# Moving the second look at two groups' decays, with its loads, to the last two groups with attention

## The chip, the cores and the metric

The kernel runs on one core of a Trainium2 chip. Its time is in device microseconds (us) and is the median of three runs of the same program. One more execution was recorded by the profiler; all rows below come from that one.

A core has five engines, each of which takes its instructions in the order in which they were written for it: TensorE (PE; PEld is its loading of weights), VectorE (DVE), ScalarE (ACT), GpSimd (POOL) and SyncE (SP). Here SP does nothing but issue DMA transfers. An instruction that waits for a semaphore holds up everything behind it on its own engine.

## The reference, cut to what matters

```python
def _attn_ref(q, k, v, alpha):            # 4 batches, 8 heads, 768 steps, 48 channels
    for t in range(S):
        state = alpha[:, :, t, :, None] * state + np.einsum('bhd,bhe->bhde', k[:, :, t], v[:, :, t])
        y[:, :, t] = np.einsum('bhd,bhde->bhe', q[:, :, t], state)

def _moe_ref(x, w_a, w_b, w_out):         # 3072 tokens, 384 -> 1536 -> 384
    return (x @ w_a) * (x @ w_b) @ w_out

def _moe2_ref(x, modality_id, w_gate, modality_bias, w1, w2):   # 8 experts, one per token
    e_idx = np.argmax(x @ w_gate + modality_bias[modality_id], axis=1)
    for e in range(E):
        h = np.maximum(x[e_idx == e] @ w1[e], 0.0)
        out[e_idx == e] = gate_w * (h @ w2[e])

def reference(...):
    y = _attn_ref(q, k, v, alpha)         # a linear attention whose state decays by alpha
    return _moe2_ref(_moe_ref(y, ...), ...)
```

## The kernel before, in words

The 3072 tokens are cut into eight groups of 384 (`NW` = 8, `WIN` = 384), and a group into three chunks of 128 (`CPW` = 3). For a group `w` the class `Attention` computes the decayed attention: a chunk's rows of alpha, k and q are loaded into tiles `raw_a`, `raw_k`, `raw_q` (eight buffers, tag "raw"), turned on DVE into `at`, `kt`, `qt`, scanned along time, and multiplied on PE: `s` are the scores, `y` the result, `u` what goes into `state`. `moe(w)` then computes the gated product of the group in twelve blocks: eighteen matmuls give `ab` (nine for each of the two factors), DVE multiplies the two factors into `g` (L632), ACT and DVE split `g` into `gh` and `gl`, and nine matmuls add to `px`. The bank of the second factor has one buffer, so the nine matmuls of the next block's second factor can't begin before DVE has read the present one into `g`.

While `moe(w)` runs, the main loop also steps through `Attention(w + 1)` and `route(w - 1)`, which picks each token's expert. From group 1 on a scheduler orders the instructions of each engine, and so it also starts a group's first chunks ahead of time: `at6_1` (group 6, chunk 1) stands beside `moe(4)`. After the eight groups the experts run, each with weights that are loaded once the routes are known.

The scans are exact only while each decay lies within 1.0 - 0.375 and 1.0 + 0.375. So every decay is also compared with these limits: `guard` (L268 and L269) takes the least and the greatest of a tile into the columns of `amin` and `amax`, and `spans()` later makes a flag of them, on which a general path hangs. For the groups 2 to 7 this is done on `at`. For the groups 0 and 1 (`LATE` = 2) it is done later: `late_guard` loads their alpha a second time in four tiles of two heads each (128 partitions of 288 numbers, 144 KB) and reduces each twice. Before, this stands at the end of the last chunk of the groups 2 and 3, beside `moe(1)` and `moe(2)`. Its tiles have the tag "sm", three buffers that the masked scores (`sm`) and the turned keys (`ktok`) use as well.

Of the kernel before, what the change touches and what calls it, by code (L numbers as in the profile page):

```python
# [10 lines left out]
F32 = mybir.dt.float32  # L11
# [4 lines left out]
ALU = mybir.AluOpType  # L16
AX = mybir.AxisListType
# [3 lines left out]
P = 128  # L21
WIN = 384
CPW = WIN // P
# [4 lines left out]
LATE = 2  # L28
# [16 lines left out]
def gla_moe_kernel(ctx, tc, q, k, v, alpha, w_a, w_b, w_out, modality_id, w_gate, modality_bias, w1, w2, out):  # L45
    nc = tc.nc
    B, H, S, D = q.shape
# [7 lines left out]
    NW = N // WIN  # L55
    WPB = S // WIN
    NPAIR = H // 2
# [66 lines left out]
    amin = const.tile([P, NW * NPAIR], F32, name="amin")  # L124
    nc.gpsimd.memset(amin, 1.0)
    amax = const.tile([P, NW * NPAIR], F32, name="amax")
# [21 lines left out]
    ap = m2 = fold = None  # L148
# [89 lines left out]
    def after_first(steps):  # L238

        gl, w = newest["gl"].ins, newest["w"].ins  # L240
        while True:
            with tc.issue_after(gl), tc.issue_after(w):
                try:
                    next(steps)
                except StopIteration:
                    return
            yield

    def behind(steps):

        while True:
            with tc.issue_after(newest["mm"].ins):
                try:
                    next(steps)
                except StopIteration:
                    return
            yield
# [8 lines left out]
    def guard(i, a):  # L266
        axis = AX.X if len(a.shape) == 2 else AX.XY
        nc.vector.tensor_reduce(amin[:, i : i + 1], a, axis=axis, op=ALU.min)  # L268
        nc.vector.tensor_reduce(amax[:, i : i + 1], a, axis=axis, op=ALU.max)  # L269

    def late_guard(w):

        b, t0 = w // WPB, (w % WPB) * WIN
        for i in range(NPAIR):
            r = ap.tile([P, 4 * P], F32, tag="sm", bufs=3, name=f"late{w}_{i}")[:, : 2 * CPW * D]
            nc.sync.dma_start(
                out=r.rearrange("p (h f) -> p h f", h=2),
                in_=alpha[b, 2 * i : 2 * i + 2, t0 : t0 + WIN, :].rearrange("h (p j) d -> p h (j d)", j=CPW),
            )
            guard(w * NPAIR + i, r)  # L280

    class Attention:

# [229 lines left out]
        def steps(self):  # L513
            w = self.w
            if w != 1:
                self.load(0)
            self.load(1)
            yield
            yield from self.prepare(0)
            for c in range(CPW):  # L520
                self.scores(c)
                yield
                ahead = self.prepare(c + 1) if c + 1 < CPW else iter(())
                yield from islice(ahead, 1)
                self.mask(c)
                yield
                yield from ahead
                self.pads(c)
                self.decay(c)
                self.values(c)  # L530
                self.halves(c)
                yield
                if self.gc(c) < S // P - 1:
                    self.keys(c)
                    self.carry(c)
                    self.add(c)
                if c == CPW - 1 and LATE <= w < 2 * LATE:
                    late_guard(w - LATE)
                yield

        def first(self, beside, second):
# [869 lines left out]
```

## Time and profile before

| | |
|---|---|
| median of three runs | 882.64 us (879.58 to 885.08) |
| the profiled execution, its own time | 880.6 us |
| its span, first to last instruction | 878.6 us |
| mean granted clock of TensorE | 0.987 of full speed |
| PE busy | 837.5 us (95%) |
| DVE busy | 633.7 us (72%) |
| ACT, POOL busy | 291.4 us (33%), 201.2 us (23%) |
| HBM read and written | 100.10 MB, 9.82 MB |

A share of busy time is a mean over stages with different limits. The groups take the span up to about 640 us, the experts the rest.

### The profile page before, as it was taken

Reading aid. Unit: us, or ns where it says so; the run is one execution under the profiler, and the core shown is the slowest. Engines: PE = TensorE matmul, PEld = TensorE weight load, DVE = VectorE, ACT = ScalarE, POOL = GpSimd, SP = SyncE. Lnnn points to the kernel's source line nnn. Section 1 sums busy time; section 2 is a strip of 40 time slices with the busy share of each in tenths; the row PEclk is TensorE's granted clock in tenths of the full one; section 3 lists DMA queues with packets and bytes.
Section 4 is the critical chain, followed back from the end, with each engine's and each line's share of the span. In section 5 each row is a group of like instructions: output and inputs, shape, how many; then the busy total and the mean of one; then the engine's idle time right before and its main releaser. Section 6 shows DMA issues by size and latency. Waiting matters only on the chain.

```text
span 878.6 us, 16754 instructions
## 1 busy us (share of the span) xinstructions
PE 837.5 (95%) x6220; PEld 782.4 (89%) x6220; DVE 633.7 (72%) x1457; ACT 291.4 (33%) x681; POOL 201.2 (23%) x273
## 2 busy tenths in 40 slices
PE   7879889989999999999999999999999999999995
PEld 6767789989998999989899998999999998998994
DVE  7799889974686888499698666356568965775651
ACT  2323332212221222222122122122465565555541
POOL 5011101120020102011100201011416554455431
PEclk9989999999999999999999999999999999999998
DMA  9989757332233313024120000100772988695810
GB/s 174 201 194 198 167 150 215 86 84 58 64 81 74 89 49 81 28 64 108 45 65 10 1 28 1 72 28 1 263 251 84 354 284 308 195 358 169 289 56 23
DMA packets 124928, 110.98 MB, mean 126 GB/s; under 512 B 55759, under 2 KB 104051, under 8 KB 124836
## 3 DMA queue, kind: packets, MB, share of 16 engines
q1 hardware_dynamic: 114548, 99.00, 40.6%
q0 software_dynamic: 4032, 9.62, 3.1%
q10 hardware_dynamic: 6256, 1.19, 1.1%
q8 instruction: 51, 0.84, 0.4%
q14 instruction: 41, 0.34, 0.1%
HBM read 100.10 MB, written 9.82 MB: 125 GB/s over the span
## 4 chain that ended last, share of the span: by engine, by line
PE 70%; DVE 13%; DMA 7%; issue 4%; POOL 2%; ACT 2%; SPq 2%; POOLq 0%; DVEq 0%; ACTq 0%
PE ab L625 26%; PE px L616 12%; PE hl L1055 8%; PE pol L1003 8%; PE s L404 3%; PE he L1055 2%; PE poe L1003 2%; DMA wa<-in_moe_w_a 2%; PE u L493 2%; DVE g L632 1%; DMA tab_d<-fill 1%; DVE at L390 1%; DVE R L379 1%; PE k L485 1%; PE y L452 1%
## 5 line engine op out<-in xcount | busy, mean ns | idle before, releaser
L625 PE MATMUL ab<-xh,pb 128*128 128x384 f32 x576 | 167.9, 345 | 10.1 <-DVE g L632 10.0
L625 PE MATMUL ab<-xh,pa 128*128 128x384 f32 x576 | 166.3, 342 | 3.4 <-DVE pa L196 2.4
L616 PE MATMUL px<-po,gh 128*128 128x384 f32 x576 | 139.6, 342 | 3.4 <-ACT gh L634 3.1
L634 ACT ACTIVATE gh<-g 128x384 fp32r<-128x384 f32 x96 | 50.3, 524 | 232.4 <-DVE g L632 223.6
L625 PEld LDWEIGHTS ab<-xh,pb 128*128 128x128 f32 x576 | 106.5, 189 | 15.5 <-DVE g L632 12.0
L625 PEld LDWEIGHTS ab<-xh,pa 128*128 128x128 f32 x576 | 105.5, 188 | 7.7 <-DVE pa L196 3.3
L632 DVE TENSOR_TENSOR g<-ab,asb 128x384 f32<-128x384 f32 x96 | 53.1, 553 | 79.2 <-PE ab L625 73.2
L616 PEld LDWEIGHTS px<-po,gh 128*128 128x128 f32 x576 | 104.3, 191 | 5.6 <-ACT gh L634 4.1
L625 PE MATMUL ab<-xl,pb 128*128 128x384 f32 x288 | 97.4, 338 | 0.0
L625 PE MATMUL ab<-xl,pa 128*128 128x384 f32 x288 | 97.1, 337 | 0.0
L630 ACT ACTIVATE asb<-ab 128x384 f32<-128x384 f32 x96 | 46.9, 489 | 146.8 <-PE ab L625 146.8
L616 PE MATMUL px<-po,gl 128*128 128x384 f32 x288 | 86.8, 340 | 0.0
L392 POOL TENSOR_TENSOR qt<-qt,at 128x512 f32<-128x512 f32 x18 | 22.2, 1235 | 254.0 <-DVE qt L358 201.5
L638 DVE TENSOR_TENSOR gl<-g,gh 128x384 fp32r<-128x384 f32 x96 | 56.2, 585 | 21.5 <-ACT gh L634 21.3
L1060 DVE SCALAR_TENSOR_TENSOR hll<-hl,hhl 128x256 fp32r<-128x256 f32 x72 | 30.3, 421 | 56.8 <-ACT hhl L1058 51.9
L671 DVE SCALAR_TENSOR_TENSOR junk<-xr,gate 128x384 bf16<-128x384 f32 x96 | 54.1, 564 | 4.8 <-ACT xr L648 3.2
L625 PEld LDWEIGHTS ab<-xl,pb 128*128 128x128 f32 x288 | 54.6, 190 | 0.1
L625 PEld LDWEIGHTS ab<-xl,pa 128*128 128x128 f32 x288 | 54.3, 188 | 0.3 <-DVE xl L479 0.2
L616 PEld LDWEIGHTS px<-po,gl 128*128 128x128 f32 x288 | 52.6, 188 | 1.0 <-issue 0.6
L437 POOL TENSOR_TENSOR state<-state,R 128x384 f32<-128x384 f32 x18 | 17.5, 970 | 135.6 <-DVE state L509 67.4
L1058 ACT ACTIVATE hhl<-hl 128x256 fp32r<-128x256 f32 x72 | 27.7, 384 | 62.1 <-PE hl L1055 53.0
L404 PE MATMUL s<-qt,kt 64*128 64x128 f32 x384 | 41.6, 298 | 4.7 <-DVE qt L392 3.9
(332 smaller groups left out, 1840.5 us busy)
## 6 DMA issues: line engine op xcount, KB each, us to landing
w1rl<-in_moe_w SPq DMA_DIRECT2D x18, 768.0 KB
w2rl<-in_moe_w SPq DMA_DIRECT2D x18, 768.0 KB
raw_a<-in_alpha SPq DMA_DIRECT2D x72, 96.0 KB
raw_k<-in_k SPq DMA_DIRECT2D x72, 96.0 KB
raw_q<-in_q SPq DMA_DIRECT2D x72, 96.0 KB
wo<-in_moe_w_out SPq DMA_DIRECT2D x6, 768.0 KB
x_d<-xr SPq DMA_DIRECT2D x24, 192.0 KB
w1re<-in_moe_w SPq DMA_DIRECT2D x6, 768.0 KB
```

The costliest lines, as they stand in the source:

```text
L404: nc.tensor.matmul(pts[g][:, i * P : (i + 1) * P], kt[o : o + 64, i, :], qt[o : o + 64, i, :], start=True, stop=True)
L616: newest["mm"] = nc.tensor.matmul(px[t][:, :DM], a_, b_, start=(f == 0 and i == 0), stop=(f == NF - 1 and i == 2))
L625: nc.tensor.matmul(pt[:, :WIN], a_, b_, start=(n == 0), stop=(n == 3 * KD - 1))
L630: nc.scalar.activation(asb, pt[:, :WIN], AF.Copy)
L632: nc.vector.tensor_tensor(g, pab[1][:, :WIN], asb, op=ALU.mult)
L634: newest["act"] = nc.scalar.activation(gh, g, AF.Copy)
L638: newest["gl"] = nc.vector.tensor_tensor(gl, g, gh, op=ALU.subtract)
L671: nc.vector.scalar_tensor_tensor(junk, xr[w][t], 1.0, gate[e], op0=ALU.mult, op1=ALU.mult, accum_out=L[:, t, e : e + 1])
L1003: newest["mm"] = nc.tensor.matmul(self.po[t][:, :DM], a_, b_, start=(f == 0 and i == 0), stop=(f == NF2 - 1 and i == 2))
L1055: nc.tensor.matmul(pt[:, :n], a_, b_, start=(i == 0), stop=(i == 3 * KD - 1))
L1058: nc.scalar.activation(gh[:, :n], pt[:, :n], AF.Relu)
L1060: nc.vector.scalar_tensor_tensor(gl[:, :n], pt[:, :n], 0.0, gh[:, :n], op0=ALU.max, op1=ALU.subtract)
```

## The change

The function `late_guard` is parted. `late_load` now loads two tiles of four heads each (128 partitions of 2 times 288 numbers, 288 KB) into buffers of the rows (tag "raw", eight of them, which don't grow), and `late_guard` reduces each tile twice, into two columns at once. The loads stand at the end of chunk 1, the reductions at the end of chunk 2, and both stand in the groups 6 and 7 in place of 2 and 3. Eight loads become four and sixteen reductions eight; the bytes stay the same.

```diff
--- before.py
+++ after.py
@@ -268,16 +268,25 @@
         nc.vector.tensor_reduce(amin[:, i : i + 1], a, axis=axis, op=ALU.min)
         nc.vector.tensor_reduce(amax[:, i : i + 1], a, axis=axis, op=ALU.max)
 
-    def late_guard(w):
+    def late_load(w):
 
         b, t0 = w // WPB, (w % WPB) * WIN
-        for i in range(NPAIR):
-            r = ap.tile([P, 4 * P], F32, tag="sm", bufs=3, name=f"late{w}_{i}")[:, : 2 * CPW * D]
+        ts = []
+        for i in range(NPAIR // 2):
+            r = ap.tile([P, 2, 2 * CPW * D], F32, tag="raw", bufs=8, name=f"late{w}_{i}")
             nc.sync.dma_start(
-                out=r.rearrange("p (h f) -> p h f", h=2),
-                in_=alpha[b, 2 * i : 2 * i + 2, t0 : t0 + WIN, :].rearrange("h (p j) d -> p h (j d)", j=CPW),
+                out=r.rearrange("p a (h f) -> p (a h) f", h=2),
+                in_=alpha[b, 4 * i : 4 * i + 4, t0 : t0 + WIN, :].rearrange("h (p j) d -> p h (j d)", j=CPW),
             )
-            guard(w * NPAIR + i, r)
+            ts.append(r)
+        return ts
+
+    def late_guard(w, ts):
+
+        for i, r in enumerate(ts):
+            cols = slice(w * NPAIR + 2 * i, w * NPAIR + 2 * i + 2)
+            nc.vector.tensor_reduce(amin[:, cols], r, axis=AX.X, op=ALU.min)
+            nc.vector.tensor_reduce(amax[:, cols], r, axis=AX.X, op=ALU.max)
 
     class Attention:
 
@@ -534,8 +543,11 @@
                     self.keys(c)
                     self.carry(c)
                     self.add(c)
-                if c == CPW - 1 and LATE <= w < 2 * LATE:
-                    late_guard(w - LATE)
+                if w >= NW - LATE:
+                    if c == CPW - 2:
+                        late = late_load(w - NW + LATE)
+                    elif c == CPW - 1:
+                        late_guard(w - NW + LATE, late)
                 yield
 
         def first(self, beside, second):
```

What the scheduler makes of it, at three places. The names carry the group first: `late0_1` is the second tile for group 0, `at3_2` the decays of group 3, chunk 2, `g1_9` the product of block 9 of `moe(1)`.

DVE beside `moe(1)`, before the change: the last rows up to the product `g1_9` (the least of `late0_0` and the turning of `at3_2` stand just ahead of them).

```order
L269 TENSOR_REDUCE amax_122<-late0_0_2090 128x1
L268 TENSOR_REDUCE amin_120<-at3_2_2646 128x1
L268 TENSOR_REDUCE amin_120<-late0_1_2094 128x1
L269 TENSOR_REDUCE amax_122<-late0_1_2094 128x1
L269 TENSOR_REDUCE amax_122<-at3_2_2646 128x1
L509 TENSOR_TENSOR state_133<-u2_2_2081,state_133 64x4x32
L509 TENSOR_TENSOR state_133<-u2_2_2081,state_133 64x4x16
L509 TENSOR_TENSOR state_133<-u2_2_2081,state_133 64x4x32
L509 TENSOR_TENSOR state_133<-u2_2_2081,state_133 64x4x16
L268 TENSOR_REDUCE amin_120<-late0_2_2098 128x1
L269 TENSOR_REDUCE amax_122<-late0_2_2098 128x1
L632 TENSOR_TENSOR g1_9_2202<-ab1_9_1_2192,asb1_9_2190 128x384
```

DVE at the same place now:

```order
L367 STREAM_TRANSPOSE at3_2_2630<-raw_a3_2_2386 128x4x4x32
L268 TENSOR_REDUCE amin_120<-at3_2_2630 128x1
L269 TENSOR_REDUCE amax_122<-at3_2_2630 128x1
L379 TENSOR_SCALAR at3_2_2630<-at3_2_2630 128x4x128
L518 TENSOR_TENSOR state_133<-u2_2_2081,state_133 64x4x32
L518 TENSOR_TENSOR state_133<-u2_2_2081,state_133 64x4x16
L518 TENSOR_TENSOR state_133<-u2_2_2081,state_133 64x4x32
L518 TENSOR_TENSOR state_133<-u2_2_2081,state_133 64x4x16
L644 TENSOR_TENSOR g1_9_2186<-ab1_9_1_2176,asb1_9_2174 128x384
```

The reductions on late tiles are gone from here (six of the eight stood ahead of `g1_9`, two a little behind it); beside `moe(2)` eight more go in the same way.

DVE beside `moe(4)`, before the change: from the turning of `qt6_0` to the product of block 6.

```order
L358 STREAM_TRANSPOSE qt6_0_4815<-raw_q6_0_4741 128x4x4x32
L358 STREAM_TRANSPOSE kt6_0_4777<-raw_k6_0_4736 128x4x4x32
L479 TENSOR_TENSOR xl5_3934<-y5_1_4310,xh5_3933 128x3x128
L358 STREAM_TRANSPOSE at6_1_4845<-raw_a6_1_4748 128x4x4x32
L388 TENSOR_TENSOR kt6_0_4777<-kt6_0_4777,R6_0_4771 128x512
L268 TENSOR_REDUCE amin_120<-at6_1_4845 128x1
L269 TENSOR_REDUCE amax_122<-at6_1_4845 128x1
L376 MEMSET R6_1_4851 128x2
L632 TENSOR_TENSOR g4_6_4458<-ab4_6_1_4448,asb4_6_4446 128x384
```

DVE at the same place now, from the turning of `kt6_0` (which stands right behind `qt6_0`):

```order
L367 STREAM_TRANSPOSE kt6_0_4745<-raw_k6_0_4704 128x4x4x32
L488 TENSOR_TENSOR xl5_3902<-y5_1_4278,xh5_3901 128x3x128
L367 STREAM_TRANSPOSE at6_1_4813<-raw_a6_1_4716 128x4x4x32
L397 TENSOR_TENSOR kt6_0_4745<-kt6_0_4745,R6_0_4739 128x512
L288 TENSOR_REDUCE amin_120<-late0_0_5108 128x2
L289 TENSOR_REDUCE amax_122<-late0_0_5108 128x2
L268 TENSOR_REDUCE amin_120<-at6_1_4813 128x1
L269 TENSOR_REDUCE amax_122<-at6_1_4813 128x1
L385 MEMSET R6_1_4819 128x2
L288 TENSOR_REDUCE amin_120<-late0_1_5110 128x2
L289 TENSOR_REDUCE amax_122<-late0_1_5110 128x2
L644 TENSOR_TENSOR g4_6_4426<-ab4_6_1_4416,asb4_6_4414 128x384
```

Four reductions on `late0` now stand ahead of `g4_6`. Beside `moe(5)` the four on `late1` stand in the same way ahead of `g5_6`, behind the turning of `at7_1`.

SP at that place, before the change:

```order
L333 DMA raw_q6_2_4828<-in_q 32x4x192 x4
L318 DMA v6_1_4763<-in_v 128x8x48
L333 DMA raw_a7_0_5534<-in_alpha 32x4x192 x4
L333 DMA raw_k7_0_5539<-in_k 32x4x192 x4
L333 DMA raw_q7_0_5544<-in_q 32x4x192 x4
L318 DMA v6_2_4833<-in_v 128x8x48
L333 DMA raw_a7_1_5551<-in_alpha 32x4x192 x4
```

SP at that place now:

```order
L342 DMA raw_q6_2_4796<-in_q 32x4x192 x4
L327 DMA v6_1_4731<-in_v 128x8x48
L277 DMA late0_0_5108<-in_alpha 128x4x144
L277 DMA late0_1_5110<-in_alpha 128x4x144
L342 DMA raw_a7_0_5510<-in_alpha 32x4x192 x4
L342 DMA raw_k7_0_5515<-in_k 32x4x192 x2
L327 DMA v6_2_4801<-in_v 128x8x48
L342 DMA raw_k7_0_5515<-in_k 32x4x192 x2
L342 DMA raw_q7_0_5520<-in_q 32x4x192 x4
```

The two loads of `late0` stand ahead of the rows of group 7. In the built program `late0_0` waits for the turning of `qt6_0` and `late0_1` for that of `kt6_0`, which free the buffers that they get; `raw_a7_0`, which got the first of these before, now waits for the turning of `at6_1`. The loads of `late1` wait in the same way for `qt7_0` and `kt7_0`.

## Rows read from the trace of the kernel before

**Rows 1.** The page, part 1 (busy time, share, instructions) and part 4 (the chain)

```profile
PE 837.5 (95%) x6220; PEld 782.4 (89%) x6220; DVE 633.7 (72%) x1457; ACT 291.4 (33%) x681; POOL 201.2 (23%) x273
...
PE 70%; DVE 13%; DMA 7%; issue 4%; POOL 2%; ACT 2%; SPq 2%; POOLq 0%; DVEq 0%; ACTq 0%
```

**Rows 2.** Idle of TensorE on the product, whole span, then 180 to 300 us

```profile
PE ab L625 <- DVE g L632: 10.0, 7, 3.4
...
PE ab L625 <- DVE g L632: 5.5, 2, 3.4
```

**Rows 3.** Timeline of PE at its two restarts: start, length, engine, line

```profile
198.87 0.44 PE L625 MATMUL ab<-xh,pb 128*128 128x384 f32 x1 [3.42 <-DVE g L632]
...
271.94 0.69 PE L625 MATMUL ab<-xh,pb 128*128 128x384 f32 x1 [2.10 <-DVE g L632]
```

**Rows 4.** Timeline of DVE at its two stops on a late load

```profile
193.90 0.45 DVE L268 TENSOR_REDUCE amin<-late 128x1 f32<-128x288 f32 x1 [3.53 <-DMA late<-in_alpha]
...
194.27 0.44 DVE L269 TENSOR_REDUCE amax<-late 128x1 f32<-128x288 f32 x1
...
269.23 0.45 DVE L268 TENSOR_REDUCE amin<-late 128x1 f32<-128x288 f32 x1 [4.59 <-DMA late<-in_alpha]
```

**Rows 5.** Windows: length; busy PE, PEld, DVE, ACT, POOL; PEclk; DMA share; GB/s

```profile
200.00:201.00 1.00, 1.00 (x6) 1.00 (x5) 1.00 (x2) 0.00 (x0) 0.00 (x0) 0.56 0.33 94
...
202.00:203.00 1.00, 1.00 (x5) 1.00 (x4) 0.96 (x3) 0.53 (x1) 0.00 (x0) 0.50 0.00 0
...
203.00:204.00 1.00, 1.00 (x6) 1.00 (x5) 0.97 (x3) 0.00 (x0) 0.00 (x0) 0.74 0.00 0
...
273.00:274.00 1.00, 1.00 (x4) 1.00 (x4) 1.00 (x4) 0.00 (x0) 0.00 (x0) 0.50 0.71 200
```

**Rows 6.** Timeline of SP: issues of loads

```profile
188.08 2.69 SPq L276 DMA_DIRECT2D late<-in_alpha  x2
...
261.74 0.38 SPq L276 DMA_DIRECT2D late<-in_alpha  x1
...
399.50 1.74 SPq L333 DMA_DIRECT2D raw_a<-in_alpha  x4
```

**Rows 7.** The tile v: its issues on SP, first and last start

```profile
L318 SPq DMA_DIRECT2D v<-in_v x23: 368/391/2347, 2.8 to 476.2; - x23
```

**Rows 8.** Window just after the last load of v

```profile
478.50:479.00 0.50, 0.50 (x4) 0.50 (x4) 0.50 (x2) 0.00 (x0) 0.00 (x0) 1.00 0.00 0
```

**Rows 9.** Timeline of DVE beside moe(4), before the product of block 6

```profile
398.37 1.11 DVE L358 STREAM_TRANSPOSE qt<-raw_q 128x512 f32<-128x512 f32 x1
...
401.73 0.67 DVE L388 TENSOR_TENSOR kt<-kt,R 128x512 f32<-128x512 f32 x1
...
402.32 0.66 DVE L268 TENSOR_REDUCE amin<-at 128x1 f32<-128x512 f32 x1
...
403.50 0.55 DVE L632 TENSOR_TENSOR g<-ab,asb 128x384 f32<-128x384 f32 x1
```

**Rows 10.** Timeline of PE beside moe(4)

```profile
407.56 0.33 PE L625 MATMUL ab<-xh,pb 128*128 128x384 f32 x1
...
420.23 0.44 PE L625 MATMUL ab<-xh,pb 128*128 128x384 f32 x1 [0.43 <-DVE g L632]
```

**Rows 11.** Timeline of DVE beside moe(5), before the product of block 6

```profile
470.04 1.14 DVE L358 STREAM_TRANSPOSE qt<-raw_q 128x512 f32<-128x512 f32 x1
...
473.30 1.06 DVE L358 STREAM_TRANSPOSE at<-raw_a 128x512 f32<-128x512 f32 x1
...
479.71 0.53 DVE L632 TENSOR_TENSOR g<-ab,asb 128x384 f32<-128x384 f32 x1
```

**Rows 12.** The chain in order of time, three pieces of PE

```profile
387.15 1.09 PE s L404 x16
...
425.84 0.42 PE s L404 x4
...
480.73 0.59 PE y L452 x8
```

## The prediction

> **What bounds the kernel now.** I read the page first: PE is busy for 95% of the span, and the chain of waits lies on PE for 70% of it, on DVE for 13% [rows 1]. So a change on DVE and SP counts only where it makes PE stand still or lets it go on. The second view is therefore what PE waits for. On the product `g` it waits 10.0 us in all, 7 times; 5.5 us of that, 2 times, lie between 180 and 300 us [rows 2], which is where the late tiles are read. The timeline of PE shows the two: 3.42 us up to 198.87, 2.10 us up to 271.94 [rows 3]. The timeline of DVE shows why: shortly before, DVE stands 3.53 and 4.59 us at a reduction of a late tile that hasn't landed [rows 4], and `g` is queued behind it, as the order of DVE shows. Last I read the granted clock: behind each of the two restarts it is at the lower of its two levels (0.50 of full speed, 1.2 GHz) for some 3 us [rows 5].
>
> **What is removed.** The two stops go with the reductions at which they happen. Worth of it: 3.42 + 2.10 = 5.52 us idle. The low clock adds what is missing to 1.00 in each window: 0.44 + 0.50 + 0.50 + 0.26 = 1.70 us from 200 to 204 (201 to 203 are two windows alike), and 3 windows of 0.50 from 272 to 275, 1.50 us [rows 5]. Together 8.7 us; the first matmuls of a restart refill the pipeline, 0.44 and 0.69 us where one takes 0.33 [rows 3, 10], and I add 0.2 us for that, 8.9 us. What is late next at the first place? Without the stop DVE has only the two reductions on `at3_2`, the clamp and the additions to `state` between the turned decays and `g1_9`; that is about 3 us of work where some 8 us passed, so `g` comes before PE asks for it. At the second place the turning of `at5_0` lies ahead of `g` as well, and needs a load that was issued in the same slow stretch; if it was no earlier than the late tile, this stop stays (a rival below). Bounds: 5.1 us (3.42 + 1.70, the first place alone) to 9.2 us (with all of that refill, 0.11 + 0.36).
>
> **What is added, in instructions.** A reduction of 288 numbers starts 194.27 - 193.90 = 0.37 us after the one before it [rows 4], one of 512 numbers 0.59 us (two of them from 402.32 to 403.50) [rows 9]. That is 0.22 us for 224 numbers, so the new ones of 576 take an estimated 0.37 + 0.28 = 0.66 us. Eight make 5.3 us, against 16 x 0.37 = 5.9 us before: DVE's sum hardly changes, its place does. Four loads fewer are issued, on SP, which waits for others there; nothing for that.
>
> **The first new place, beside moe(4).** The loads are written a chunk ahead of the reductions, but a load can start only when its buffer is free. SP issued `raw_a7_0` at 399.50 [rows 6], at the end of the turning of `qt6_0` (398.37 + 1.11) [rows 9]. Now `late0_0` waits for just that, so it starts at 399.5. DVE reaches its first reduction where it now reduces `at6_1`, at 402.32 [rows 9]: the load has 2.8 us. Two bounds for its landing. With nothing ahead of it, the last load of `v` (192 KB) was issued at 476.2 [rows 7] and the DMA was quiet from 478.5 on [rows 8]: 2.3 us. The late loads of 144 KB took 193.88 - 188.08 = 5.8 us and 269.2 - 261.74 = 7.5 us from issue to the reduction that waited [rows 4, 6], both with other loads right before them. SP's queue is empty at 399.5 as it was at 476.2, so I take the near end: some 2.8 us for 288 KB, no stop.
>
> The Trainium skill gives a price for the same thing: "DMA: Bandwidth & Descriptors", section "Anatomy of one DMA", has about 2.0 us fixed and the bytes by 436 GB/s, which makes an estimated 2.7 us for 288 KB. By it the load is just in time and the sum stands as it is; the 5.8 and 7.5 us of the late loads are rows against it, and by them the first rival holds.
>
> Then `g4_6` is done at 402.32 + 2 x 0.66 + 1.18 + 2 x 0.66 + 0.55 = 406.7; PE asks for it at 407.56 [rows 10]. The margin is 0.9 us, and where the load lands later than 403.2, PE waits. DVE is 2.6 us behind from here on, with little idle time before the next product on which PE waits already, 0.43 us at 420.23 [rows 10]; I let that wait grow by 0.5 us. Cost of this place: 0.5 us.
>
> **The second new place, beside moe(5).** `qt7_0` is turned by 470.04 + 1.14 = 471.2, DVE is through `at7_1` at 474.36 [rows 11]: 3.2 us for the load. `g5_6` is then done at 474.36 + 1.32 + 1.18 + 1.32 + 0.55 = 478.7, before that 480.2, since the additions to `state`, the masks and a scan move behind it. The masks come some 2.6 us later for it, but PE now has a group of nine `ab` matmuls and six `px` matmuls ahead of `y`, which began at 480.73 [rows 12]. No cost.
>
> **A by-product.** The scheduler splits the scores of groups 3 to 7 into fewer pieces (34 before, 30 now, with one piece more each of `y`, `u` and `k`). A quarter of a chunk's scores takes 0.42 us by itself, where all of them take 1.09 [rows 12], that is 0.27 a quarter; four pieces less give back 4 x (0.42 - 0.27) = 0.6 us, the three others take some of it. I count 0.5 us; between 0 and 1.2.
>
> **The sum.** -8.9 + 0.5 + 0 - 0.5 = -8.9 us. The best bounds are -9.2 + 0 + 0 - 1.2 = -10.4; the worst ones are the slower rival's. The profiled execution took 880.6 us, so 871.7 for one like it; the median of the runs is 2.0 us above it, and I predict that: 882.6 - 8.9 = 873.7. Everything behind the groups (routes, loads of weights, experts) hangs on their end and moves with it.
>
> **The rivals.**
> - The wait moves along. DVE stands at `late0_0` and `late1_0` as it did before, with a landing of 5.8 us: stops of 3.0 and 2.6 us. For it speaks that the buffer sets the start and leaves 2.8 us, against it the empty queue. At the first place `g` is done at 409.7, PE idles 2.1 us, and 2.10 us of idle were enough for the low clock before: 1.5 us more. At the second, PE is there at some 480.7 and `g` at 481.3: 0.6 us. Sum 4.2 us above the forecast: 878.
> - The same on the other side: slower than before. With landings of 7.5 us at both places the stops are 4.7 and 4.3 us, PE idles 3.8 and 2.3 us, each with 1.6 us of low clock, and DVE beside `moe(4)` is over 7 us behind, with 2 to 3 us more at 420. Together 3.8 + 1.6 + 2.3 + 1.6 + 2.5 = 11.8 us, against 8.9 + 0.5 won, 2.4 above the time before: 885. It decides from a landing of about 6.9 us at both.
> - Only half goes. At the second old place another load is as late as the late tile, and 2.10 + 1.5 us stay: 877.
> - More comes back. PE's other waits on `g`, 10.0 - 5.5 = 4.5 us [rows 2], shrink with the new order; nearly all of it gone gives 870.
>
> **How the numbers follow.** Chances: forecast 0.54, the wait moves along 0.23, only half 0.10, more comes back 0.08, slower 0.05. The range of 869 to 881 holds the forecast and the three cases about it, each with an edge of 1 us or more (the three runs before lie up to 3 us from their median), and leaves out the slower rival. One per cent, 8.8 us, is about what a measurement of this kernel can tell from no change, and the forecast lies on that edge: about half of its chance (0.28) and all of the case in which more comes back (0.08) are faster by over 1%, 0.36. Slower by over 1% begins at 891.5, 6 us above the slower rival: 0.03. Within 1% is the rest, 0.61.
>
> **What would show it.** In the profile of the changed kernel there is no wait of PE on `g` above 1 us and no low clock between 180 and 300; DVE's reductions of late tiles begin with no idle time before them; SP issues `late0_0` right behind the turning of `qt6_0`; PE's wait near 412 (420 less the gain) is below 1.5 us. I am wrong if DVE stands for over 1 us at `late0_0` or `late1_0`, or if PE's idle time near 190 or 265 stays under another name.

## The result, and the profile after

The changed kernel takes 873.33 us (median of 7 runs, 871.87 to 875.40) where the kernel before takes 881.74 us in the same comparison (7 runs). The ratio is 0.9899, with a 95% interval of 0.9877 to 0.9920: some 8.9 us of 881.7, between 7.1 and 10.8. The forecast was 873.7 us.

The page of the changed kernel, its head and part 1, and then what PE waits for in the whole span (waited for, us in total, times, longest):

```profile
span 870.5 us, 16735 instructions
...
PE 834.4 (96%) x6220; PEld 780.2 (90%) x6220; DVE 636.5 (73%) x1449; ACT 291.6 (34%) x681; POOL 202.8 (23%) x273
```

```profile
PE ab L637 <- DVE g L644: 4.5, 6, 1.7
```

DVE does the same work as before, within 3 us [rows 1]. PE's wait on `g` falls from 10.0 to 4.5 us [rows 2]; between 180 and 300 us PE waits for nothing any more. The two windows below, in which PE comes to the second factor of block 10 of `moe(1)` (at 196.34) and of block 9 of `moe(2)` (at 265.53), are full and at the upper clock; there the kernel before stood 3.42 and 2.10 us [rows 3] and then ran at 0.50 [rows 5].

```profile
196.00:197.00 1.00, 1.00 (x7) 1.00 (x7) 0.96 (x4) 0.41 (x1) 0.00 (x0) 1.00 0.71 198
...
265.00:266.00 1.00, 1.00 (x9) 0.88 (x10) 0.90 (x2) 0.49 (x1) 0.00 (x0) 1.00 0.62 138
```

The loads at their new place, in the timeline of SP (start, length of the issues together), and DVE there:

```profile
392.51 1.31 SPq L277 DMA_DIRECT2D late<-in_alpha  x2
...
462.84 1.78 SPq L277 DMA_DIRECT2D late<-in_alpha  x2
```

```profile
391.37 1.11 DVE L367 STREAM_TRANSPOSE qt<-raw_q 128x512 f32<-128x512 f32 x1
...
395.33 0.74 DVE L288 TENSOR_REDUCE amin<-late 128x2 f32<-128x576 f32 x1
395.98 0.74 DVE L289 TENSOR_REDUCE amax<-late 128x2 f32<-128x576 f32 x1
...
399.16 0.55 DVE L644 TENSOR_TENSOR g<-ab,asb 128x384 f32<-128x384 f32 x1
...
466.67 0.75 DVE L288 TENSOR_REDUCE amin<-late 128x2 f32<-128x576 f32 x1 [0.55 <-DMA late<-in_alpha]
...
470.51 0.55 DVE L644 TENSOR_TENSOR g<-ab,asb 128x384 f32<-128x384 f32 x1
```

`late0_0` is issued as the turning of `qt6_0` ends and has landed when DVE gets to it, 395.33 - 392.51 = 2.8 us later. `late1_0` takes 466.67 - 462.84 = 3.8 us, and DVE stands 0.55 us for it. SP had issued nothing since 445.40 there, so its queue was as empty as at the first place; why this load took 1 us longer, no run shows. A reduction of 576 numbers starts 0.65 us after the one before. The timeline of PE shows when the product is asked for:

```profile
400.56 0.33 PE L637 MATMUL ab<-xh,pb 128*128 128x384 f32 x1
...
412.84 0.44 PE L637 MATMUL ab<-xh,pb 128*128 128x384 f32 x1 [0.48 <-DVE g L644]
...
472.22 0.33 PE L637 MATMUL ab<-xh,pb 128*128 128x384 f32 x1
...
531.27 0.44 PE L637 MATMUL ab<-xh,pb 128*128 128x384 f32 x1 [0.92 <-DVE g L644]
```

`g4_6` is done at 399.71, 0.85 us before 400.56, and `g5_6` at 471.06, 1.2 us before 472.22. The wait that was 0.43 us at 420.23 [rows 10] is now 0.48 us. The one of 0.92 us at 531.27 lies beside `moe(6)`, where the kernel before waits 1.30 us on `g`.

How long each group takes shows where the time went. The table gives, worked out from the timeline of DVE, the time from the product of block 0 of `moe(w)` to that of `moe(w + 1)`, in us, for all kernels of this study; "gain" is the difference of the sums, and "by runs" is (1 - ratio) x 881.7.

| kernel | moe(1) | moe(2) | moe(3) | moe(4) | moe(5) | moe(6) | sum | gain | by runs |
|---|---|---|---|---|---|---|---|---|---|
| before | 79.34 | 81.69 | 71.95 | 75.68 | 71.70 | 69.38 | 449.74 | | |
| before, once more | 79.31 | 80.96 | 71.96 | 75.70 | 71.69 | 69.39 | 449.01 | 0.7 | |
| changed | 74.02 | 79.49 | 71.40 | 75.96 | 70.32 | 68.31 | 439.50 | 10.2 | 8.9 |
| no second look | 74.01 | 79.49 | 71.40 | 75.62 | 71.70 | 69.40 | 441.62 | 8.1 | 6.6 |
| new form, groups 2, 3 | 74.76 | 79.48 | 71.40 | 75.72 | 71.70 | 69.41 | 442.47 | 7.3 | 6.6 |
| old form, groups 6, 7 | 74.03 | 79.48 | 71.40 | 75.62 | 70.49 | 69.39 | 440.41 | 9.3 | 6.6 |
| first look alone moved | 74.03 | 81.85 | 71.96 | 76.03 | 70.59 | 66.25 | 440.71 | 9.0 | 6.8 |
| second look alone moved | 79.83 | 79.48 | 71.40 | 75.72 | 72.92 | 69.39 | 448.74 | 1.0 | 3.5 |
| new form, groups 4, 5 | 74.02 | 78.35 | 71.21 | 75.63 | 72.07 | 69.02 | 440.30 | 9.4 | 8.1 |
| reductions twice over | 74.07 | 79.49 | 71.40 | 76.27 | 78.25 | 67.88 | 447.36 | 2.4 | 1.0 |
| groups 6 and 4 | 74.02 | 78.35 | 71.07 | 76.16 | 70.59 | 66.60 | 436.79 | 12.9 | 13.0 |
| groups 6 and 3 | 74.05 | 79.49 | 71.40 | 76.16 | 70.59 | 66.26 | 437.95 | 11.8 | 10.3 |
| old form, rows' buffers | 76.41 | 79.49 | 71.40 | 75.72 | 71.70 | 69.39 | 444.11 | 5.6 | 7.5 |

Each row comes from one profiled execution. A cell in which nothing has changed repeats from program to program within 0.1 us as long as TensorE's clock does (`moe(2)` of the kernel before is an exception, see the last section), which makes the table finer than the run times. What lies outside it (`moe(0)`, the experts) doesn't repeat so well, and makes up the differences of up to 3 us between the last two columns.

### The profile page after: what moved, and what is told of

Its sections match the earlier page's. It is cut to its first block, busy times and chain, and to the rows that moved or that the text cites. A ratio compares the mean times of both kernels' runs of the same rounds, so it can differ in the third digit from the quotient of the medians.

```text
span 870.5 us, 16735 instructions
## 1 busy us (share of the span) xinstructions
PE 834.4 (96%) x6220; PEld 780.2 (90%) x6220; DVE 636.5 (73%) x1449; ACT 291.6 (34%) x681; POOL 202.8 (23%) x273
## 3 DMA queue, kind: packets, MB, share of 16 engines
q10 hardware_dynamic: 6256, 1.19, 1.1%
## 5 line engine op out<-in xcount | busy, mean ns | idle before, releaser
L637 PE MATMUL ab<-xh,pb 128*128 128x384 f32 x576 | 165.8, 341 | 4.6 <-DVE g L644 4.5
```

The lines of the kernel that those rows point to most:

```text
L637: nc.tensor.matmul(pt[:, :WIN], a_, b_, start=(n == 0), stop=(n == 3 * KD - 1))
```

## The experiments

**What the look costs in all.** The changed kernel without the second look; `spans()` reads the groups 2 to 7 alone.

```diff
-                if w >= NW - LATE:
-                    if c == CPW - 2:
...
+        nc.vector.tensor_reduce(span[:, 0:1], amin[:, LATE * NPAIR :], axis=AX.X, op=ALU.min)
```

> This kernel leaves out the second look at the first two groups' decays (loads and reductions), so the flag is made from the groups 2 to 7 alone. It shows what the look costs in all. Theory (the two stops beside moe(1) and moe(2) were the cost, and the look is free at its new place): as fast as the changed kernel within 1.5 us, 872 to 875 us; the scores are split into four pieces more than in the changed kernel, as in the kernel before, which is worth some 0.6 us against it. Rival (the look still costs something at its new place, since DVE is 2.6 us behind there): 868 to 870 us, and PE's waits on g of 2.2 us between 380 and 480 us are gone.

Measured: 875.12 us, ratio 0.9925 (0.9897 to 0.9953). The rival is out: without the look the kernel is not faster. By the table it is 2.1 us slower, all of it in `moe(4)` to `moe(6)`, which are as long as before. So by the table (the intervals of the two ratios overlap) the changed kernel gains more than the whole price of the look, and 2.1 us of its gain don't come from the stops.

**Form without place.** The loads and reductions of the changed kernel at the groups 2 and 3.

```diff
-                if w >= NW - LATE:
+                if LATE <= w < 2 * LATE:
...
```

> The new form (two tiles of four heads each in the buffers of the rows, loaded a chunk ahead) at the old groups 2 and 3. Theory (the place decides, since loads queue behind the rows of the next chunks there): DVE stands 1 to 4 us at one or both of the looks, PE waits on g between 130 and 300 us, 876 to 882 us. Rival (the form decides: fewer and wider transfers and reductions, from buffers that come free earlier): no stop, 872 to 874 us.

Measured: 875.33 us, ratio 0.9925 (0.9901 to 0.9949): between the two, and the view of the late tiles speaks for the rival (first and last start in us; idle time of DVE before them would stand under the line on it, which is empty):

```profile
L277 SPq DMA_DIRECT2D late<-in_alpha x4: 368/388/451, 131.7 to 176.0; - x4
L288 DVE TENSOR_REDUCE amin<-late x4: 725/738/751, 135.4 to 181.2; 128x2 f32<-128x576 f32 x4
```

DVE doesn't stand. The loads begin at 131.7 and 175.1 us where before the first load of each look began at 188.1 and 253.2: with the rows' buffers the scheduler puts them ahead of the rows of the next chunks, not behind. At `moe(1)` 4.6 of the 5.3 us are won; `moe(2)` to `moe(6)` are as in the kernel without the look.

**Place without form.** The kernel before with its four small tiles at the groups 6 and 7.

```diff
-                if c == CPW - 1 and LATE <= w < 2 * LATE:
-                    late_guard(w - LATE)
+                if c == CPW - 1 and w >= NW - LATE:
+                    late_guard(w - NW + LATE)
```

> The old form (four tiles of two heads each with the tag sm, each load right ahead of its reductions) at the new groups 6 and 7. Theory (the place decides): no PE wait on g above 1.7 us, 872 to 876 us. Rival (the form decides): DVE stands 3 to 4 us at each group's first late tile and PE 2 to 3 us behind it, with low clock after it, 878 to 884 us.

Measured: 874.61 us, ratio 0.9925 (0.9898 to 0.9952). The place alone does it too. DVE still stands, beside `moe(6)`, but shorter, and PE doesn't wait for it:

```profile
548.24 0.45 DVE L268 TENSOR_REDUCE amin<-late 128x1 f32<-128x288 f32 x1 [2.24 <-DMA late<-in_alpha]
...
551.74 0.45 DVE L268 TENSOR_REDUCE amin<-late 128x1 f32<-128x288 f32 x1 [1.07 <-DMA late<-in_alpha]
```

**The buffers alone.** One tag in the kernel before, with the tile's size that it needs.

```diff
-            r = ap.tile([P, 4 * P], F32, tag="sm", bufs=3, name=f"late{w}_{i}")[:, : 2 * CPW * D]
+            r = ap.tile([P, 2 * 2 * CPW * D], F32, tag="raw", bufs=8, name=f"late{w}_{i}")[:, : 2 * CPW * D]
```

> The kernel before with one word changed: its four small late tiles take the tag of the rows (eight buffers) in place of the tag sm (three, shared with the masked scores and turned keys). Loads, reductions and groups stay. Theory (the buffers decide: only the wait for the three shared buffers put the loads behind the rows of the next chunks; with the rows' buffers the scheduler puts them some 28 rows earlier in SP's order): no stop at a late tile and no PE wait on g above 1.7 us, 874 to 877 us, as with the new form at the old groups. Rival (the width of the tiles is needed too): DVE stands 2 us or more at a late tile, 878 to 882 us.

Measured: 878.05 us against 885.47 us of the kernel before on that chip, ratio 0.9915 (0.9891 to 0.9940), which is 874 us on the scale of the others. The first late load starts at 132.8 us (188.1 before) and stands 61 issues earlier on SP, and the longest stop at a late tile is 0.50 us:

```profile
L276 SPq DMA_DIRECT2D late<-in_alpha x8: 368/386/419, 132.8 to 181.7; - x8
...
182.18 0.45 DVE L268 TENSOR_REDUCE amin<-late 128x1 f32<-128x288 f32 x1 [0.50 <-DMA late<-in_alpha]
```

So the tag, three buffers shared with other tiles, was what put the loads into the slow stretch; neither wider tiles nor another group is needed to be rid of it. That the scheduler placed them late because those buffers came free late is likely, but no run shows it by itself. Nor does a run show why loads took 5.8 and 7.5 us to land in that stretch: a row load or two right ahead is not enough, since in the run of the new form at the groups 2 and 3 a late load of twice the size right behind four of them landed in 3.1 us. The windows show only that the DMA engines were busy there and moved little (the last two figures are their share and GB/s); the first is of the kernel before, the second of this run:

```profile
189.00:190.00 1.00, 1.00 (x8) 1.00 (x7) 1.00 (x2) 0.00 (x0) 0.00 (x0) 1.00 0.90 75
...
133.00:134.00 1.00, 1.00 (x8) 1.00 (x7) 1.00 (x2) 0.17 (x1) 0.00 (x0) 1.00 0.77 196
```

`moe(1)` stays 2.4 us longer than in the changed kernel: PE waits 1.7 us more there (1.5 us of it on the routing of `moe(0)`), and in this execution the granted clock is at 0.50 to 0.67 from 162 to 166 (last section).

**One look at a time.** First the look at group 0 alone, then the look at group 1 alone, in the new form; the other stays as it was. (`small_guard` is `late_guard` of the kernel before.)

```diff
+                if c == CPW - 1 and w == LATE + 1:
+                    small_guard(1)
+                if w == NW - LATE:
...
```

> Only the look at group 0 is moved (new form, beside moe(4)); that at group 1 stays as it was, beside moe(2). Theory (two stops that add up, each with its low clock): the wait of 3.4 us and its low clock are gone, that of 2.1 us and its low clock stay, 875.5 to 878 us. Rival (the stops are linked, the second takes up what the first no longer holds back): the wait at the second place grows to 4 us or more, 879 to 882 us.

Measured: 875.15 us, ratio 0.9923 (0.9896 to 0.9950). The stops add up: `moe(1)` loses 5.3 us, `moe(2)` stays, with its wait:

```profile
267.75 0.45 PE L650 MATMUL ab<-xh,pb 128*128 128x384 f32 x1 [2.18 <-DVE g L657]
```

What was not expected: `moe(4)` to `moe(6)` together are 3.9 us shorter than before, more than in the changed kernel (2.2 us).

```diff
+                if c == CPW - 1 and w == LATE:
+                    small_guard(0)
+                if w == NW - 1:
...
```

> Only the look at group 1 is moved (new form, beside moe(5)); that at group 0 stays as it was, beside moe(1). Theory (the two stops add up): the wait of 3.4 us and its low clock stay, that of 2.1 us and its low clock go; 876.5 to 880 us, with moe(1) at 79.3 us and moe(2) at 79.5 us from product to product.

Measured: 881.99 against 885.47 us, ratio 0.9960 (0.9940 to 0.9980), or 878.2 on the common scale. `moe(2)` and `moe(3)` are as forecast, `moe(1)` keeps its stop. But `moe(5)` is 1.2 us longer than before: the late tile lands 0.72 us after DVE gets to it, and PE then waits for the masks, which now stand behind the reductions:

```profile
201.26 0.44 PE L650 MATMUL ab<-xh,pb 128*128 128x384 f32 x1 [3.92 <-DVE g L657]
...
474.75 0.75 DVE L288 TENSOR_REDUCE amin<-late 128x2 f32<-128x576 f32 x1 [0.72 <-DMA late<-in_alpha]
...
481.36 0.66 PE L472 MATMUL y<-qt,state 128*64 128x128 f32 x8 [0.96 <-DVE sm L444]
```

So by the table the look beside `moe(4)` brings time, and that beside `moe(5)` costs some.

**How much room there is.** Every late tile of the changed kernel is reduced twice over.

```diff
             nc.vector.tensor_reduce(amin[:, cols], r, axis=AX.X, op=ALU.min)
             nc.vector.tensor_reduce(amax[:, cols], r, axis=AX.X, op=ALU.max)
+            nc.vector.tensor_reduce(amin[:, cols], r, axis=AX.X, op=ALU.min)
+            nc.vector.tensor_reduce(amax[:, cols], r, axis=AX.X, op=ALU.max)
```

> The changed kernel with every late tile reduced twice over (eight reductions of some 0.65 us more, 5.2 us of DVE; transfers unchanged). Theory (DVE beside moe(4) and moe(5) has about 1 us to spare before each group's sixth product and room behind it): at moe(4) no wait, at moe(5), where four more reductions, the additions and the masks now stand ahead of the product of block 6, PE waits 1 to 4 us; 874 to 879 us. Rival (DVE's added time is free there altogether): 872 to 874 us. Rival (every us of DVE counts): 878.5 us.

Measured: 882.57 us, ratio 0.9989 (0.9958 to 1.0020), which is 880.7 us on the common scale (878.0 to 883.5): worse than the first two expectations, while 878.5 us for the third lies just inside the interval. By the table it is worse than that one too: 5.2 us of DVE cost 7.9 us, all of it beside `moe(5)`, 78.25 where the changed kernel has 70.32. Again PE waits for the masks, not for the product, and the clock falls behind the wait:

```profile
479.62 0.69 PE L463 MATMUL y<-qt,state 128*64 128x128 f32 x4 [3.04 <-DVE sm L435]
```

```profile
478.00:479.00 1.00, 0.00 (x0) 0.00 (x0) 1.00 (x3) 0.00 (x0) 0.00 (x0) 1.00 0.00 0
479.00:480.00 1.00, 0.38 (x4) 0.41 (x6) 1.00 (x4) 0.03 (x1) 0.00 (x0) 0.53 0.00 0
480.00:481.00 1.00, 1.00 (x16) 0.65 (x16) 1.00 (x1) 0.88 (x2) 0.00 (x0) 0.50 0.00 0
```

The wait (3.04 us) and the low clock (1.7 us) are 4.7 of the 7.9 us. The rest goes with another order: the scores there are cut 2, 4, 2, 4, 2, 2 in place of 4, 6, 6. DVE's time beside `moe(5)` is not free; in the changed kernel PE doesn't wait for the masks yet.

**Other groups.** The new form at 4 and 5; then at 6 for group 0 and at 4 or 3 for group 1.

```diff
-                if w >= NW - LATE:
+                if 4 <= w < 4 + LATE:
...
```

> The changed kernel with the look at the groups 4 and 5 in place of 6 and 7 (everything else as in the changed kernel). First theory (the queue of loads is empty only beside the last two groups): DVE stands over 2 us at a late tile beside moe(2) or moe(3), with a wait of PE on g and low clock, 878 us or more. Second theory (any place does where the loads don't stand behind the last chunk's rows; what the changed kernel has beyond that comes from the new order of PE beside moe(4) to moe(6)): no stop, moe(4) to moe(6) as long as before (75.7, 71.7 and 69.4 us from product to product), 874 to 876.5 us.

Measured: 874.35 us, ratio 0.9908 (0.9874 to 0.9942), no stop at a late tile. The second theory holds: `moe(4)` to `moe(6)` are as before (216.7 us together, before 216.8).

```diff
-                if w >= NW - LATE:
+                if w in (6, 4):
                     if c == CPW - 2:
-                        late = late_load(w - NW + LATE)
+                        late = late_load({6: 0, 4: 1}[w])
...
```

> The look at group 0 at group 6 as in the changed kernel, that at group 1 at group 4, both in the new form. Theory (the stops are gone wherever the loads stand early, and PE's order beside moe(4) to moe(6) is best with one look only there, as in the run with only the first look moved: 66.3 us of moe(6) where before has 69.4): 870 to 872.5 us, faster than the changed kernel by 1 to 3 us. Rival (what was seen there belongs to the disturbed moe(2) of that kernel): as the changed kernel, 873 to 874.5 us.

Measured: 869.22 us (868.67 to 870.60, 6 runs), ratio 0.9853 (0.9813 to 0.9893). Each of these runs lies below each of the changed kernel's, but in another comparison, whose kernel before was slower (883.73 us), and the two intervals of the ratio overlap a little. The table has it 2.7 us faster: 1.5 us from `moe(2)` and `moe(3)`, 1.2 us from `moe(4)` to `moe(6)`. PE's waits on `g` fall by another 1.1 us:

```profile
PE ab L637 <- DVE g L644: 3.4, 4, 1.7
```

> The look at group 0 at group 6 as in the changed kernel, that at group 1 at group 3, both in the new form. Theory: as with groups 6 and 4, 870 to 872.5 us, with up to 0.6 us for the late tile beside moe(1). Rival: as the changed kernel, 873 to 874.5 us.

Measured: 872.26 us, ratio 0.9883 (0.9841 to 0.9925), 1.6 us faster than the changed kernel by the table, 1.1 by the medians, which the runs alone can't tell from nothing. What the two have in common is that nothing is added beside `moe(5)`.

**The kernel before once more.**

> The kernel before once more, for a second profile of it. Theory (the first 40 us, where the first loads land, and the experts' stage differ by 1 to 2 us from one execution to the next; the groups 1 to 6 don't): the products of the groups 1 to 6 come at the same distances as in the first profile within 0.1 us, all shifted by up to 2 us; 879 to 884 us.

Measured: 885.44 us on the slower chip, span 883.5. `moe(1)` and `moe(3)` to `moe(6)` repeat within 0.03 us, as expected; `moe(2)` is 0.7 us shorter, though PE waits longer there (last section). `moe(0)` was 3.1 us longer in this execution, 2 of them with a low clock from 100 to 107 us that the first profile doesn't have. The first profile was a good one: in all twelve others of this study `moe(1)` begins later, by 0.2 to 3.6 us. The changed kernel's profile loses 1.1 us against it before `moe(1)` and as much behind the first product of `moe(7)`, so that of the 10.2 us in the table 8.1 are left between the two spans.

## Why the prediction was right, step by step

- **The two stops (8.9 us).** Right in mechanism and size. `moe(1)` is 5.3 us shorter (3.42 idle, 1.70 clock, 0.1 refill). At the second stop the low clock cost 1.5 us: the second execution of the kernel before, which didn't have it, waits 0.76 us longer there and is still 0.73 us shorter. (The 0.69 us of the first matmul there, which the prediction took for refill, was mostly this clock; at the upper clock it is 0.44.) That makes 2.10 + 1.5 + 0.1 = 3.7 us, but at `moe(2)` and `moe(3)` only 2.75 us are gone. The other 0.95 us is a remainder that no run measures alone; it goes with a new order there (one piece of `k` and two of `y` more in the two groups together), which the prediction had lumped into the by-product. The feared second load was no later than the late tile.
- **The first new place (0.5 us cost).** The load was forecast at some 2.8 us and took at most 2.8. The price of the Trainium skill ("DMA: Bandwidth & Descriptors", "Anatomy of one DMA"), which that section fits to transfers issued by GpSimd, gave an estimated 2.7 us; these loads are issued by SyncE. The trace of this place doesn't contradict it, and at the second place a load of the same size took 3.8 us. The margin at `g4_6` was forecast at 0.9 us and is 0.85. PE's wait behind it, which was forecast to grow by 0.5 us, is 0.05 us longer.
- **The second new place (no cost).** This step was wrong. The lead of 3.2 us did not cover a landing of 3.8, and the sentence that PE has enough ahead of `y` to outlast the later masks failed: with this look alone moved, PE waits 0.96 us on the masks and `moe(4)` to `moe(6)` are 1.3 us longer; taking it away from there gives 1.6 us (groups 6 and 3). In the changed kernel itself it isn't the masks: 1.2 of the 1.6 us are waits on `g`, 0.30 us at 490.32 and the 0.92 us at 531.27, neither of which the run with the groups 6 and 3 has.
- **The by-product (0.5 us, between 0 and 1.2).** Too small. Without the other look beside `moe(5)`, that beside `moe(4)` brings 3.4 to 3.9 us (three runs). Of it 1.1 us are waits of PE on `g` (3.4 us in `moe(4)` to `moe(6)` before and in the changed kernel, 2.3 to 2.4 in these runs). Another 1.6 us are pieces of the scores. The timeline of PE of the changed kernel shows their price:

```profile
264.62 0.34 PE L637 MATMUL ab<-xh,pa 128*128 128x384 f32 x1
264.89 0.71 PE L413 MATMUL s<-qt,kt 64*128 64x128 f32 x6
265.53 0.45 PE L637 MATMUL ab<-xh,pb 128*128 128x384 f32 x1
265.81 0.34 PE L637 MATMUL ab<-xl,pb 128*128 128x384 f32 x1
...
270.80 0.34 PE L637 MATMUL ab<-xh,pa 128*128 128x384 f32 x1
271.06 0.49 PE L413 MATMUL s<-qt,kt 64*128 64x128 f32 x4
271.49 0.44 PE L637 MATMUL ab<-xh,pb 128*128 128x384 f32 x1
271.77 0.34 PE L637 MATMUL ab<-xl,pb 128*128 128x384 f32 x1
```

Two matmuls of `ab` without a piece between them start 0.175 us apart. From 270.80 to 271.77 two such steps take 0.97 us, so the piece of four costs 0.97 - 0.35 = 0.62 us; the one of six costs 1.19 - 0.35 = 0.84. A piece of two costs as much as one of four (0.61 us at each of 14 places, 0.62 at each of 13, in the changed kernel and the one without the look). The prediction took 0.42 against 0.27 us for a quarter, 0.15 us for a piece, from the length of the rows alone; the gap ahead and the slow restart, which the rows above show, belong to it. Beside `moe(4)` and again beside `moe(5)` the chunk that was split 4, 2, 4, 2, 4 (3.1 us) is now split 4, 6, 6 (2.3 us), so that each of the two cuts that are gone was worth some 0.4 us. The pieces of the one beside `moe(5)`, in the kernel before and then in the changed one:

```profile
493.75 0.49 PE L404 MATMUL s<-qt,kt 64*128 64x128 f32 x4
...
497.53 0.48 PE L404 MATMUL s<-qt,kt 64*128 64x128 f32 x2
...
499.73 0.49 PE L404 MATMUL s<-qt,kt 64*128 64x128 f32 x4
...
503.51 0.48 PE L404 MATMUL s<-qt,kt 64*128 64x128 f32 x2
...
505.71 0.49 PE L404 MATMUL s<-qt,kt 64*128 64x128 f32 x4
```

```profile
493.67 0.49 PE L413 MATMUL s<-qt,kt 64*128 64x128 f32 x4
...
499.00 0.71 PE L413 MATMUL s<-qt,kt 64*128 64x128 f32 x6
...
504.53 0.71 PE L413 MATMUL s<-qt,kt 64*128 64x128 f32 x6
```

About 1 us of the look's gain beside `moe(4)` I can't attribute.
- **The sum.** By the table 5.3 + 2.75 + 2.2 = 10.2 us in the groups, where 8.9 was the forecast. Two errors cancel in part: 1.3 to 1.6 us too little cost beside `moe(5)`, and some 3 us too little gain by the new order beside `moe(4)`. The runs give 8.9 us with an interval of 7.1 to 10.8, which doesn't tell the two sums apart. That 873.7 came within 0.4 us of the median is therefore luck in part; the main term is not.
- **What the prediction didn't see** is that the move wasn't needed for its main term: the rows' buffers alone, or the place alone, or the wide form at the old place each take PE's stops away. The loads were late because their tag put them into a stretch in which they landed slowly. And the lead of a chunk in the code isn't needed for that: in the run with the buffers alone the loads are still written right ahead of their reductions.

## What to carry to other kernels

When a load stops an engine, look first at which buffer it waits for: a tag shared with tiles that live on the critical path can put a load tens of issues further back in the queue (61 here), and changing the tag is a smaller edit than moving the work. Small matmuls that are put between long ones cost a fixed part for each interruption (here 0.61 us for two and 0.62 us for four), so a scheduler's cuts (4, 2, 4, 2, 4 against 4, 6, 6) are worth counting on both sides of a change. And a place for extra work isn't free because the product behind it is in time: everything else behind it on that engine, here the masks, has a reader too.

## What the runs showed of the hardware

The granted clock didn't fall after every wait of the same kind. In the second execution of the kernel before PE stood longer at the same matmul of `moe(2)` than in the first [rows 3], and its clock stayed up. Its timeline of PE, and then windows of it behind both waits:

```profile
202.45 0.48 PE L625 MATMUL ab<-xh,pb 128*128 128x384 f32 x1 [3.42 <-DVE g L632]
...
276.26 0.44 PE L625 MATMUL ab<-xh,pb 128*128 128x384 f32 x1 [2.86 <-DVE g L632]
```

```profile
277.00:278.00 1.00, 1.00 (x8) 1.00 (x7) 1.00 (x3) 0.14 (x1) 0.00 (x0) 1.00 0.65 176
...
203.00:204.00 1.00, 1.00 (x4) 1.00 (x4) 1.00 (x4) 0.34 (x1) 0.00 (x0) 0.50 0.85 228
```

2.10 us of idle were followed by 1.5 us of loss, 2.86 us by none (the clock is at 1.00 from 276 to 281), 3.42 us by a loss both times. The prediction's sentence that 2.10 us are enough for the low clock holds for one execution and not for the next. So a stop of 2 to 3 us has a price that differs by 1.5 us between runs of one program.

A shorter wait shows the same: PE's matmul `k` that waits for the routing of `moe(0)`, in the run of the new form at the groups 2 and 3 and in that with the buffers alone.

```profile
160.51 0.66 PE L494 MATMUL k<-ident,kt 128*128 128x128 f32 x4 [1.59 <-DVE L L698]
...
162.31 1.11 PE L485 MATMUL k<-ident,kt 128*128 128x128 f32 x4 [1.53 <-DVE L L686]
```

Behind the first the clock stays at 1.00; behind the second it is at 0.50 to 0.67 up to 166, and `moe(1)` is 1.65 us longer.
